# Seven products for the last pair of f blocks in groups 2 and 3, too: S form from the k stage, T forms kept in DRAM

## The chip, the cores and the metric

The kernel runs on one core of a Trainium2 chip. The core has a matrix engine (TensorE, PE in the profile; its weight loads are PEld), VectorE (DVE), ScalarE (ACT), GpSimd (POOL) and SyncE (SP). The last two issue most of the transfers here. Each engine works through its own queue of instructions in order and waits on semaphores for the others. Matmuls write into PSUM, eight banks of 128 x 512 fp32 values; everything else lies in SBUF, or in DRAM.

The metric is the device time of one execution in microseconds. Before the change it is 728.93 us, the median of three runs (728.89 to 728.98).

## The reference

The input x has 2048 tokens of 640 features. The output is a mix, with a gate for each token, of two blocks:

```
g = sigmoid((x * gate_w).sum(-1))
a = linear attention of x (32 heads of 20): phi(q), phi(k), v from x @ wqkv,
    o = (phi(q) @ (phi(k)^T v)) / (phi(q) . sum phi(k)),  a = o @ wo
h = sigmoid(x @ w_gate) * (x @ w_up)        # 640 -> 1536
b = h @ w_down                              # 1536 -> 640
out = g * a + (1 - g) * b
```

All is fp32. The change concerns b in its last step, `h @ w_down`, for half of the tokens.

## The kernel before

**Three matmuls for a product.** The matrix engine takes the type fp32r, which keeps fewer bits of an fp32 value. So each operand is split into a high part (`hi`, a rounded copy that ScalarE makes) and a low part (`lo`, the rest, which VectorE subtracts), and `mm3` issues hi x hi, hi x lo and lo x hi into the same bank. `split` is that pair of instructions.

**Groups and blocks.** The tokens form four groups of 512 (`TG`), which the kernel treats in pairs: the call with `pr = 1` treats groups 2 and 3, that with `pr = 0` groups 0 and 1. The k stage comes first (keys, and the sums that linear attention needs), over chunks of 256 tokens of two groups at once. Then come `q_phase(1)` and `f_phase(1)`, then `q_phase(0)` and `f_phase(0)`, then the attention output. `f_phase` runs over 12 blocks f of 128 hidden features (`FC`). A block has steps 1 to 7, which compute gate and up products for both groups of the pair, and a tail, which forms h = sigmoid(gate) * up.

**Seven products for eight.** Two groups times two weights make a 2 x 2 block product, which is computed with seven products in place of eight from sums of the operands. On the x side these sums are the T forms (`Chunk.sum`, `Chunk.form`: four of them, in SBUF tiles `xt`), on the weight side the S forms. The down products do the same: two f blocks are a pair p, whose h tiles are B11, B12, B21, B22 (first digit: block; second: group), with the sums T1 to T4 of these, and the weights' sums S1 to S4, each for two of the five output blocks at a time (q = 0 and 1); the fifth output block (W and V in the code) takes plain products. `down_pair` is a generator that issues the products of a pair in the order in which the code names them; each `yield` hands back to `f_phase`, which puts a step of the next blocks in between. `new` starts a bank, `go` adds a product to it, `seed` copies a bank to another one on ScalarE, and `out` adds a bank to the sum `tb` on VectorE. For three outputs of the last pair of groups 0 and 1 (`FAR`), `far` copies the bank on ScalarE instead and adds it to `tb` by an accumulating DMA from GpSimd.

**The last pair (blocks 10 and 11).** In groups 0 and 1 it runs behind block 11 with the seven products. In groups 2 and 3, `last_down` runs it with plain products: for ten outputs (five output blocks, two groups) the terms of block 10 and of block 11. The first four outputs start with block 10's terms while block 11's h is being made. `tail_f` makes the h tiles for this. `last_down` also multiplies each output by 1 - g (`scaled`, with `omg` in the tile `ds`) and stores it in `b_dram`.

**Weights.** For groups 2 and 3 the raw w_down block is loaded (`load_d`, tile `dst`), split (`split_d`, tile `wd`) and stored in `wd_dram` for the other groups; for pairs 0 to 4 `queue_ds` and `queue_df` make the S forms (tile `ds`), and store them also. Pair 5's S form is needed for groups 0 and 1 alone; `queue_last_s` makes it in `f_phase(0)`, and `load_last_s` loads it before the last pair.

**x for the next pair.** During the last blocks of `f_phase(1)`, x of groups 0 and 1 is loaded again in two chunks (`other`), and its plain splits (`queue_a`, `queue_b`, `plain_b12`) and T forms (`queue_both`: four sums and four forms for each chunk) are made during the last pair and the first q products. The k stage had made the same T forms for its own use.

**Who sets the order.** All queues are filled in one program order, and `Order` plans it: a model of the time at which TensorE, ScalarE and VectorE come to each instruction. Products are issued in the order of the code. Work on the other two engines is either issued at its place in the code (tails, seeds, outs) or queued by `order.add`; `order.fill` issues queued work where it fits within a slack of TensorE's time, streams with a due time when that comes near, and `order.need(key)` issues all that a product is about to use. The k stage has a list of `kept` items, the pieces of three q weights, that `order.run("qw")` issues one by one at fixed places. `Ring.dma_start` keeps the same kind of account for SP's and GpSimd's transfers.

Of the kernel before, what the change touches and what calls it, by code (L numbers as in the profile page):

```python
# [27 lines left out]
EPS = 1e-6  # L28

# [344 lines left out]
def gated_mix_kernel(ctx: ExitStack, tc: tile.TileContext, xt, xn, wk, wv, wo, wst_q, wst_f, out_t):  # L374
# [160 lines left out]
    class Chunk:  # L535
# [67 lines left out]
        def form(self, t):  # L603
            split(*self.f.t_part(t, self.cs), self.T[t])
# [62 lines left out]
    chunks[0].b12 = (b12h, b12l)  # L667
    wk_st = [op_tile(t, F32) for t in ("xnh", "xnh", "xnl", "pkh", "pkl")]
# [65 lines left out]
    w_dram = {}  # L734
# [311 lines left out]
    for c in range(1, 4):  # L1046
# [496 lines left out]
    wd_dram = {}  # L1543
# [9 lines left out]

    def split_d(n):
# [5 lines left out]
        def rest():  # L1560
            if j == 0:
                wd_dram[p] = dram.tile([P, 2, WF], F32, name=f"wd{p}")
            gp.dma_start(wd_dram[p][:, :, (1 - j) * D:(2 - j) * D], f32(t))
            if p == FC // 2 - 1:
                load_d()
        order.then(rest)
# [45 lines left out]
    WF = 2 * D + 8 * P  # L1612
# [9 lines left out]
    def wf_tile():  # L1622
        return down_pool[1].tile([P, 2, WF], F32R, name="wf", tag="wf")

# [51 lines left out]
    def queue_last_s():  # L1676

        p, w = FC // 2 - 1, 4 * P
        raw = [down_pool[1].tile([P, D], F32, name=n, tag=n)[:, :w] for n in ("mr", "mv")]
        for j in range(2):  # L1680
            sp.dma_start(raw[j], wst_f[2 * p + j, :, 2, :w])
        (a11, a21), (a12, a22) = [r.rearrange("p (q h c) -> h p q c", q=2, h=2) for r in raw]
        at = lambda: max(order.when(r) for r in raw) + 1
        ready = [at]

        def sums(part):
            if part == 0:
                add(a22, a21, a22)
                sub(a21, a11, a21)
            else:  # L1690
                sub(a11, a22, a11)
                sub(a12, a12, a11)

        def form(j):
            t = down_pool[1].tile([P, 2, D], F32R, name="mt", tag="mt")[:, :, :w]
            split(t[:, 0], t[:, 1], raw[j])
            dst = wd_dram[p][:, :, 2 * D + j * w:2 * D + (j + 1) * w]
            ready[0] = lambda: 1e9

            def rest():  # L1700
                gp.dma_start(dst, f32(t))
                ready[0] = lambda: order.when(dst) + 12
            order.then(rest)
        for part in range(2):
            order.add(0, 2 * v_cost(2 * P), lambda part=part: sums(part), "m", at, spare=True)
        for j in range(2):
            order.add(a_cost(w), v_cost(w), lambda j=j: form(j), "m", lambda: ready[0](), spare=True)

    def m_close():
# [13 lines left out]
        other.append(Next(0, 1, xf, CW, c1_x, True))  # L1723

# [50 lines left out]

    def tail_f(f, blk, late=False):
        def t3():
            h_split(f, 0, blk.c11, "v")

        def t4():  # L1780
            act(blk.c12, blk.c12, AF.Sigmoid, "v")
            vec2(blk.c12, blk.c22, blk.c12, OP.mult, "a")

        def t5():
            if late:
                order.add(a_cost(TG), v_cost(TG), lambda: h_split(f, 1, blk.c12, ""), ("hl", f))
            else:
                h_split(f, 1, blk.c12, "v")
        return {3: t3, 4: t4, 5: t5}
# [87 lines left out]
    FAR = [(FC // 2 - 1, 4, 0), (FC // 2 - 1, 0, 0), (FC // 2 - 1, 2, 0)]  # L1877

    def down_pair(pr, p):
# [26 lines left out]
        def far(key, o, g):  # L1906
            if not far_at:
# [7 lines left out]
        def out(key, o, g):  # L1915
            dst = tb[:, o, g]
            if not pr and (p, o, g) in FAR:
# [8 lines left out]

        if p == FC // 2 - 1:
# [18 lines left out]
            go("X0", "S2", "T2")  # L1946
            out("X0", 0, 1)
            go("X1", "S2", "T2", q=1)
            out("X1", 2, 1)
            go("Z0", "S4", "B22")  # L1950
            out("Z0", 0, 1)
            go("Z1", "S4", "B22", q=1)
            out("Z1", 2, 1)
            go("X0", "S3", "T3")
            seed("U0", "rot", "X0")
            out("X0", 1, 1)
            go("X1", "S3", "T3", q=1)
            seed("U1", "rot", "X1")
            out("X1", 3, 1)
            go("W", "w1", "B22")  # L1960
            out("W", 4, 1)
# [5 lines left out]
        if pr:  # L1967
            for j in range(2):
                order.need(("d", ("f", 1, 2 * p + j)))
# [143 lines left out]
    def f_phase(pr, q, hooks={}):  # L2113
# [10 lines left out]
        if pr:  # L2124
            order.plan[pr, FC + 1, "d0"] = at - EARLY
        else:
            for s, n in (("d1", 1), (3, 8), ("d2", 13), ("d3", 15)):
                order.plan[pr, FC + 1, s] = at + mm * n

        def step(f, s):  # L2130
# [24 lines left out]
            if s == 7:  # L2155
                tails[f] = tail_f(f, blk, f == FC - 2) if pr and f >= FC - 2 else tail_s(f, blk) if f < FC - 1 else tail_last(f, blk)
# [28 lines left out]
        for f in range(FC):  # L2185
# [29 lines left out]
            else:  # L2215
                if not pr:
                    queue_t1(f // 2)
# [3 lines left out]
            if f % 2 and f < FC - 1:  # L2221
                queue_t1(f // 2)
                if pr:
                    if f > 1:
                        queue_df(f // 2)
                    queue_d(("f", 1, f + 1))
# [3 lines left out]
            elif not pr:  # L2230
# [10 lines left out]
    def last_down(pr, units):  # L2241
        order.need(("d", ("f", pr, FC - 1)))
        order.need(("hl", FC - 2))
        early = {}
        order.slack_a, order.slack_v = 0.6, 0.8
        if True:
            omg = f32(down_pool[1].tile([P, 2, 8 * P], F32R, name="ds", tag="ds"))[:, :, :TG]
            for g in range(2):
                sp.dma_start(omg[:, g], gate_dram[1, (2 + g) * TG:(3 + g) * TG].partition_broadcast(P))
# [5 lines left out]

        for i in units[:4]:
            g, o = divmod(i, KC)
            early[i] = ps_tile("rot" if (o + g) % 2 else "dd")
            down_term(early[i], pr, FC - 2, o, g, True)
        for i in units:  # L2260
            g, o = divmod(i, KC)
            down_unit(pr, FC - 2, o, g, early.pop(i, None))
            order.add(0, v_cost(TG), lambda i=i: scaled(i), ("tb", i),
                      lambda: order.vec + 0.6, lazy=True)
            order.fill()
        order.slack(False)
# [32 lines left out]
    def load_forms(kind, f, *forms):  # L2299
# [474 lines left out]
```

## Time and profile before

| What | Value |
|---|---|
| median of three runs | 728.93 us |
| the profiled execution | 728.59 us |
| its span | 726.9 us, 10146 instructions |
| granted TensorE clock | 1.000 |
| DMA packets | 74137, 176.95 MB, mean 243 GB/s |

The span is the time between the first and the last instruction of the profiled execution. A row of a timeline has the start and the duration in us, the engine, the line of the code (often that of a helper: 406 to 408 are the three matmuls of `mm3`, 419 is `act`, 423 is `vec2`), the operation, the tile written and those read, the shape, how many instructions the row stands for, and in brackets the idle time before it with what ended it. Durations of instructions that follow each other overlap a little, so the distance between starts tells the pace. The last pair of groups 2 and 3 lies at 392 to 406 us, the last pair of groups 0 and 1 at 645 to 657 us, and the k stage before 135 us.

### The profile page before, as it was taken

The page shows a single profiled execution, that of the slowest core. Times are in us where ns is not written, and L with a number is a line of the kernel's source. Part 1 is how long each engine was busy: PE and PEld are TensorE (multiplying, and loading weights), DVE is VectorE, ACT ScalarE, POOL GpSimd, SP SyncE. Part 2 cuts the span into 40 slices and gives each one's busy share as a digit, 9 for nine tenths or more (in the row PEclk, how much of TensorE's full clock was granted, in tenths as well). Part 3 has the DMA queues.
Part 4 walks back from the last instruction along what each step waited for, and adds up shares of the span by engine and source line. Part 5 has one row for each costly group of instructions (what it writes and reads, how often), then busy time and mean ns, then how long its engine had stood idle before and what let it go on. Part 6 is the DMA issues. An engine that isn't in the chain of part 4 may idle for free.

```text
span 726.9 us, 10146 instructions
## 1 busy us (share of the span) xinstructions
PE 722.2 (99%) x3563; PEld 620.8 (85%) x3563; DVE 573.0 (79%) x1006; ACT 364.0 (50%) x675; POOL 101.2 (14%) x166
## 2 busy tenths in 40 slices
PE   9999999999999999999999999999999999999997
PEld 8999999988888888888888888888888888888886
DVE  6889778987687889898989973447585968698895
ACT  6884649357656653535355363454333232354451
POOL 0211101113212211211210031001000001212000
PEclk9999999999999999999999999999999999999999
DMA  8665658698787866567687289879799695979612
GB/s 258 160 181 111 184 130 252 151 338 295 268 313 259 332 223 232 194 223 253 255 322 273 94 295 331 312 233 311 238 329 358 213 363 169 309 280 291 245 59 102
DMA packets 74137, 176.95 MB, mean 243 GB/s; under 512 B 11834, under 2 KB 35402, under 8 KB 70502
## 3 DMA queue, kind: packets, MB, share of 16 engines
q1 hardware_dynamic: 56102, 111.56, 47.7%
q0 software_dynamic: 17840, 64.57, 25.3%
q8 instruction: 28, 0.46, 0.3%
q14 instruction: 23, 0.19, 0.1%
q10 hardware_dynamic: 144, 0.16, 0.1%
HBM read 105.53 MB, written 64.97 MB: 235 GB/s over the span
## 4 chain that ended last, share of the span: by engine, by line
PE 99%; DVE 0%; issue 0%
PE ch L406 11%; PE ch L407 11%; PE ch L408 11%; PE cc L406 9%; PE cc L407 9%; PE cc L408 9%; PE dd L406 7%; PE dd L408 7%; PE dd L407 7%; PE rot L406 6%; PE rot L407 6%; PE rot L408 6%; PE rot L1505 1%; PE rot L494 0%; PE ch L2576 0%; PE cc L2576 0%
## 5 line engine op out<-in xcount | busy, mean ns | idle before, releaser
L419 ACT ACTIVATE c<-ch 128x512 f32<-128x512 f32 x52 | 31.1, 598 | 90.6 <-PE ch L408 90.5
L423 DVE TENSOR_TENSOR hf<-c,hf 128x512 fp32r<-128x512 f32 x78 | 53.1, 687 | 21.5 <-ACT hf L419 21.2
L419 ACT ACTIVATE hf<-c 128x512 fp32r<-128x512 f32 x78 | 47.7, 625 | 26.0 <-DVE c L423 26.0
L423 DVE TENSOR_TENSOR c<-cc,c 128x512 f32<-128x512 f32 x40 | 27.6, 689 | 34.5 <-PE cc L408 22.3
L406 PE MATMUL ch<-xth,ws 128*128 128x512 f32 x112 | 43.7, 390 | 0.0
L408 PE MATMUL ch<-xth,ws 128*128 128x512 f32 x112 | 43.6, 389 | 0.0
L407 PE MATMUL ch<-xtl,ws 128*128 128x512 f32 x112 | 43.6, 389 | 0.0
L423 DVE TENSOR_TENSOR tb<-rot,tb 128x512 f32<-128x512 f32 (+1 forms) x61 | 39.1, 675 | 3.0 <-PE rot L408 3.0
L423 DVE TENSOR_TENSOR c<-c,c 128x512 f32<-128x512 f32 x50 | 34.4, 688 | 3.3 <-ACT c L419 2.7
L406 PE MATMUL dd<-xrh,wg 128*128 128x512 f32 x90 | 35.2, 391 | 0.0
L408 PE MATMUL dd<-xrh,wg 128*128 128x512 f32 x90 | 35.0, 389 | 0.0
L407 PE MATMUL dd<-xrl,wg 128*128 128x512 f32 x90 | 35.0, 389 | 0.0
L419 ACT ACTIVATE c<-dd 128x512 f32<-128x512 f32 x22 | 13.2, 598 | 41.1 <-PE dd L408 41.1
L423 DVE TENSOR_TENSOR tb<-dd,tb 128x512 f32<-128x512 f32 x40 | 27.4, 686 | 7.7 <-PE dd L408 7.6
L406 PE MATMUL cc<-xbh,ws 128*128 128x512 f32 x84 | 32.7, 389 | 0.0
L408 PE MATMUL cc<-xbh,ws 128*128 128x512 f32 x84 | 32.7, 389 | 0.0
L407 PE MATMUL cc<-xbl,ws 128*128 128x512 f32 x84 | 32.7, 389 | 0.0
L419 ACT ACTIVATE dd<-ch 128x512 f32<-128x512 f32 x22 | 12.8, 582 | 33.6 <-PE ch L408 33.6
L423 DVE TENSOR_TENSOR wst<-wst 128x256 f32<-128x256 f32 (+2 forms) x69 | 27.4, 413 | 1.4
L408 PEld LDWEIGHTS ch<-xth,ws 128*128 128x128 f32 x112 | 21.0, 188 | 4.7
L407 PEld LDWEIGHTS ch<-xtl,ws 128*128 128x128 f32 x112 | 21.0, 188 | 4.2
L406 PEld LDWEIGHTS ch<-xth,ws 128*128 128x128 f32 x112 | 21.0, 188 | 4.1
(663 smaller groups left out, 2362.1 us busy)
## 6 DMA issues: line engine op xcount, KB each, us to landing
wf<-ws POOLq DMA_DIRECT2D x12, 1152.0 KB, 7.6
ws<-wf SPq DMA_DIRECT2D x11, 1152.0 KB, 8.6
wst<-wst_f SPq DMA_DIRECT2D x12, 640.0 KB, 5.1
wf<-wg POOLq DMA_DIRECT2D x12, 640.0 KB, 6.9
wd<-wd POOLq DMA_DIRECT2D x12, 640.0 KB, 8.0
wg<-wf SPq DMA_DIRECT2D x12, 640.0 KB, 5.7
wf<-wd SPq DMA_DIRECT2D x10, 640.0 KB, 9.2
xnst<-xn SPq DMA_DIRECT2D x16, 320.0 KB, 4.2
```

The lines of the kernel that those rows point to most:

```text
L406: nc.tensor.matmul(out, l_hi, r_hi, start=first, stop=False, skip_group_check=True)
L407: nc.tensor.matmul(out, l_hi, r_lo, start=False, stop=False, skip_group_check=True)
L408: nc.tensor.matmul(out, l_lo, r_hi, start=False, stop=last, skip_group_check=True)
L419: nc.scalar.activation(out, src, fn, **kw)
L423: nc.vector.tensor_tensor(out, a, b, op=op)
L1505: nc.tensor.matmul(ps[:w, :w], v[:, m, :w], gt[:, m, c0:c0 + w], start=(m == 0), stop=(m == KC - 1))
```

## The change

- `last_down` and `tail_f` go. Groups 2 and 3 run the last pair through `last_pair` and `down_pair`, as groups 0 and 1 do, in an order of its own: Z0 and Z1 come later, W is finished earlier, R0 and R1 are copies of X0 and X1, so that U0 and U1 start from those, and other banks are used. `FAR` holds for both, with other tiles in groups 2 and 3.
- `queue_ls` makes pair 5's S form in the k stage: two raw loads, four sums in two items, four splits with a store each. They follow the q pieces in the `kept` list, and the places at which the k stage issues these are changed. `queue_last_s` goes. `load_last_s` now runs for both pairs of groups.
- `Chunk.form` stores the T forms of the k stage's second chunk (`chunks[1]`) in `xt_dram`; `load_t` loads them in front of the last pair, and the sums and forms of that chunk are no longer queued.
- The stores of the split weights of blocks 10 and 11 (`last_stores`) and the load of the last raw q block come behind or into the pair; the loads of two q weights come behind the T loads. The scaling by 1 - g (`queue_scaled`) moves into `q_phase(0)`, with its gate rows loaded by GpSimd.

```diff
         def form(self, t):
-            split(*self.f.t_part(t, self.cs), self.T[t])
+            f = self.f.t_part(t, self.cs)
+            split(*f, self.T[t])
+            if self is chunks[1]:
+                order.then(lambda: [gp.dma_start(xt_dram[:, t, i], f32(f[i])) for i in range(2)])
...
+    def queue_ls():
+
+        p, w = FC // 2 - 1, 4 * P
+        wd_dram[p] = dram.tile([P, 2, WF], F32, name=f"wd{p}")
+        raw = qs.tile([P, 2, D], F32, name="qraw", tag="qraw")[:, :, :w]
+        for j in range(2):
+            sp.dma_start(raw[:, j], wst_f[2 * p + j, :, 2, :w])
...
+        def form(j, q):
+            cs = slice(j * w + 2 * q * P, j * w + 2 * (q + 1) * P)
+            t = qs.tile([P, 2, 2 * P], F32R, name="qp", tag="qp", bufs=2)
+            split(t[:, 0], t[:, 1], raw[:, j, 2 * q * P:2 * (q + 1) * P])
+            order.then(lambda: sp.dma_start(wd_dram[p][:, :, 2 * D + cs.start:2 * D + cs.stop], f32(t)))
+        for part in range(2):
+            order.add(0, 2 * v_cost(2 * P), lambda part=part: sums(part), "qw", None, kept=True)
+        for j in range(2):
+            for q in range(2):
+                order.add(a_cost(2 * P), v_cost(2 * P), lambda j=j, q=q: form(j, q), "qw", None, kept=True)
...
-            if c > 1 and n in (2, 5,):
+            for _ in range(({1: 1, 2: 1, 3: 1, 5: 1}, {3: 2, 4: 1, 5: 1})[c - 2].get(n, 0) if c > 1 else 0):
                 order.run("qw")
...
+            if c == 2 and u == 9:
+                queue_ls()
...
+    def load_last_s(pr=1):
+
+        p = FC // 2 - 1
+        if pr:
+            t = down_pool[1].tile([P, 2, 8 * P], F32R, name="ds", tag="ds")
+            DS[p] = [t[:, c] for c in range(2)]
+        else:
+            DS[p] = [x2_tile("ds", F32R).rearrange("p a b -> p (a b)") for _ in range(2)]
+        for c in range(2):
+            sp.dma_start(f32(DS[p][c]), wd_dram[p][:, c, 2 * D:])
...
+    def load_t(t):
+        c = other[1]
+        for i, f in enumerate(c.f.t_part(t, c.cs)):
+            sp.dma_start(f32(f), xt_dram[:, t, i])
...
         if p == FC // 2 - 1:
+            tags = ("cc", "ch") if pr else ("ch", "ch")
             new("W", "dd", "w0", "B11")
-            new("X0", "ch", "A11", "B11")
+            new("X0", tags[0], "A11", "B11")
             seed("V", "dd", "W")
+            yield
             new("X1", "ch", "A11", "B11", 1)
             seed("Y0", "rot", "X0")
             seed("Y1", "rot", "X1")
             yield
-            new("Z0", "cc", "S1", "T1")
-            out("Z0", 1, 1)
-            new("Z1", "cc", "S1", "T1", 1)
-            out("Z1", 3, 1)
+            def zs():
+                new("Z0", "ch" if pr else "cc", "S1", "T1")
+                out("Z0", 1, 1)
+                new("Z1", "cc", "S1", "T1", 1)
+                out("Z1", 3, 1)
+            if not pr:
+                zs()
             go("V", "w1", "B21")
...
             go("W", "w0", "T1")
...
+            if pr:
+                zs()
+                go("W", "w1", "B22")
+                out("W", 4, 1)
+            for q in range(2):
+                go(f"X{q}", "S2", "T2", q=q)
+                if pr:
+                    seed(f"R{q}", "rot", f"X{q}")
+                out(f"X{q}", 2 * q, 1)
+            for q in range(2):
+                go(f"Z{q}", "S4", "B22", q=q)
+                out(f"Z{q}", 2 * q, 1)
+            for q in range(2):
+                x = f"R{q}" if pr else f"X{q}"
+                go(x, "S3", "T3", q=q)
+                seed(f"U{q}", tags[q] if pr else "rot", x)
+                out(x, 2 * q + 1, 1)
+            if pr:
+                order.need((nx[1], 2))
+                order.need(("wg", ("q", 0, 4)))
+            else:
+                go("W", "w1", "B22")
+                out("W", 4, 1)
             go("U0", "A22", "T4")
...
-    def last_down(pr, units):
...
+    def last_pair(pr, tail, between):
+
+        down = down_pair(pr, FC // 2 - 1)
+        order.slack_a = order.slack_v = -9.0
+        if pr:
+            order.need((nx[1], None))
+            next(down)
+        tail[4]()
+        if not pr:
+            next(down)
+        next(down)
+        tail[5]()
+        order.slack_a, order.slack_v = 0.6, 0.8
+        for name in ("T3", "T4"):
+            queue_h(FC // 2 - 1, name)
+        between()
+        for _ in down:
+            pass
+        order.slack(False)
...
-        (FC - 1, 7): [lambda: load_forms("q", 0, 1, 2), queue_b],
+        (FC - 1, 7): [lambda: [load_t(t) for t in (1, 0, 2, 3)], queue_b],
     })
     nx = other
-    for s in (3, 4, 5):
-        tail[s]()
-    for c in other:
-        order.add(a_cost(2 * CW), v_cost(2 * CW), c.plain_b12, (nx[1], "plain"))
-    queue_both(nx)
-    queue_q(4)
-    last_down(1, range(2 * KC))
...
+    def next_x():
+        load_d()
+        load_forms("q", 0, 1, 2)
+        for c in other:
+            order.add(a_cost(2 * CW), v_cost(2 * CW), c.plain_b12, (nx[1], "plain"))
+        w = 2 * CW
+        c = other[0]
+        for ns, t, k in (((0, 1, 2), 1, 3), ((), 0, 4), ((), 2, 5), ((3,), 3, 6)):
+            for m in ns:
+                order.add(0, v_cost(w), lambda m=m: c.sum(m), None, lambda: c.at)
+            order.add(a_cost(w), v_cost(w), lambda t=t: c.form(t), (nx[1], k))
+        queue_q(4)
+    last_pair(1, tail, next_x)
+    for fn in last_stores:
+        fn()
```

More of the change, by code (lines that the diff above doesn't have):

```diff
@@ L1674, in queue_m @@
         order.add(a_cost(D), v_cost(D), fn, "m", lambda: order.when(raw) + 2, spare=True)
[L1676 to L1707, printed above, removed]
     def m_close():
@@ L1906, in far @@
         def far(key, o, g):
-            if not far_at:
+            if not far_at and order_pr[0]:
+                t = f32(wd_tile())
+                far_at.extend((t[:, 0], t[:, 1], down_pool[1].tile([P, D], F32, name="far", tag="dst", bufs=2)))
+            elif not far_at:
                 far_at.extend(down_pool[1].tile([P, D], F32, name="far", tag=n) for n in ("mr", "mv"))
@@ L1945, in down_pair @@
             go("W", "w0", "T1")
[L1946 to L1961, printed above, removed]
+            if pr:
[18 more added lines that the diff above has]
+                order.need(("wg", ("q", 0, 4)))
+            else:
+                go("W", "w1", "B22")
+                out("W", 4, 1)
             go("U0", "A22", "T4")
@@ L2229, in f_phase @@
                 step(f + 1, 2)
-            elif not pr:
+            else:
                 tail_last(f, blocks[f])[3]()
@@ L2254, in scaled @@
             gp.dma_start(b_dram[:, o, g], tb[:, o, g])
[L2256 to L2262, printed above, removed]
+        for i in range(2 * KC):
             order.add(0, v_cost(TG), lambda i=i: scaled(i), ("tb", i),
-                      lambda: order.vec + 0.6, lazy=True)
-            order.fill()
-        order.slack(False)
+                      lambda: max(order.vec + 0.6, order.when(omg)), lazy=True)
     order.need((nx[1], 2))
@@ L2526, in gated_mix_kernel, with next_p @@
     })
-    down = down_pair(0, FC // 2 - 1)
-    order.slack_a = order.slack_v = -9.0
-    tail[4]()
-    next(down)
-    tail[5]()
-    order.slack_a, order.slack_v = 0.6, 0.8
-    for name in ("T3", "T4"):
-        queue_h(FC // 2 - 1, name)
-    load_p(groups[1])
-    for g in groups[:2]:
-        load_b(g)
-    for _ in down:
-        pass
-    order.slack(False)
+    def next_p():
+        load_p(groups[1])
+        for g in groups[:2]:
+            load_b(g)
+    last_pair(0, tail, next_p)
     for u in range(KC):
```

90 lines of the change are left out of this document (40 added, 50 removed).

## The prediction

> **What bounds the kernel now.** I read the page's busy times first, then the waits of TensorE, then the windows and timelines around the last pair of groups 2 and 3, because the page alone does not say how full the other engines are there.
>
> ```profile
> PE 722.2 (99%) x3563; PEld 620.8 (85%) x3563; DVE 573.0 (79%) x1006; ACT 364.0 (50%) x675; POOL 101.2 (14%) x166
> ...
> PE rot L494 <- PEq L2765: 0.8, 1, 0.8
> ...
> 380.00:400.00 20.00, 20.00 (x90) 16.56 (x89) 18.96 (x32) 9.68 (x18) 1.42 (x3) 1.00 0.77 286
> 400.00:420.00 20.00, 20.00 (x95) 16.80 (x94) 18.28 (x30) 8.40 (x15) 0.56 (x1) 1.00 0.32 114
> 420.00:440.00 20.00, 20.00 (x90) 16.56 (x89) 14.20 (x23) 11.45 (x21) 9.35 (x18) 1.00 0.89 302
> ```
>
> Busy times and waits say the same: TensorE is the bound from end to end, and its one wait (0.8 us) is the first instruction. The windows (columns PE, PEld, DVE, ACT, POOL, clock, DMA share, GB/s) say what is second: around the change VectorE works 18.96 and 18.28 of 20 us. So a matmul taken out is time gained, and whatever makes VectorE or a load late there gives it back.
>
> The stretch that is replaced, in TensorE's timeline:
>
> ```profile
> 389.76 0.39 PE L408 MATMUL cc<-hf,ds 128*128 128x512 f32 x1
> ...
> 391.80 0.39 PE L408 MATMUL cc<-xbh,ws 128*128 128x512 f32 x1
> 392.03 0.39 PE L406 MATMUL dd<-hf,wd 128*128 128x512 f32 x1
> ...
> 405.63 0.39 PE L406 MATMUL ch<-xah,wg 128*128 128x512 f32 x1
> ```
>
> last_down runs from 392.03 to 405.63: 20 products of three matmuls, so 60 in 13.60 us, 0.2267 us each, without a gap.
>
> **The matmuls.** down_pair issues 18 products for the last pair (W three times, V, Y0, Y1, R0, R1, U0, U1 once, X0, X1, Z0, Z1 twice), so 54 matmuls in place of 60: 6 x 0.2267 = 1.36 us less, 0.187%. Nothing else on TensorE changes, in the k stage or in groups 0 and 1 (the same 18 products in the same order). Since TensorE has no gap to close, 1.36 us is all that can be gained, and the rest of the sum is what is given back. The Trainium skill ("TensorE: Matmul & The Clock Gate", section "Part 1: The HAM clock gate") gives N/2.4 GHz + 2.5 ns between starts, 215.7 ns for 512 columns; by that the six are worth an estimated 1.29 us and the sum would be 0.07 us longer. The trace differs, with 226.7 ns, and decides.
>
> **A model for the stretch.** The same seven products already run at the end of groups 0 and 1, so their hand-overs have rows (TensorE, ScalarE, VectorE):
>
> ```profile
> 654.50 0.39 PE L408 MATMUL ch<-hf,ds 128*128 128x512 f32 x1
> ...
> 646.13 0.63 ACT L419 ACTIVATE c<-c 128x512 f32<-128x512 f32 x1 [2.30 <-DVE c L423]
> 646.67 0.58 ACT L419 ACTIVATE dd<-dd 128x512 f32<-128x512 f32 x1
> 647.18 1.03 ACT L419 ACTIVATE rot<-ch 128x512 f32<-128x512 f32 x2
> ...
> 654.99 1.26 ACT L419 ACTIVATE rot<-ch 128x512 f32<-128x512 f32 x2 [2.50 <-PE ch L408]
> ...
> 645.41 0.69 DVE L423 TENSOR_TENSOR c<-cc,c 128x512 f32<-128x512 f32 x1 [0.48 <-PE cc L408]
> ```
>
> The sigmoid of c12 starts 0.72 us after the c12 sum (645.41 to 646.13); the copies that seed a bank follow it 0.54 us later and each other at 0.51, and take 0.58; a seed starts 0.49 us after its source's last matmul (654.50 to 654.99). One product takes 0.68 us. So in the new order, with t = 0 at 392.03, the products are due at: W 0, X0 0.68, X1 1.36, V 2.04, Y0 2.72, Y1 3.40, W with T1 4.08, Z0 (S1) 4.76, Z1 5.44, W with B22 6.12, X0 and X1 (S2) 6.80 and 7.48, Z0 and Z1 (S4) 8.16 and 8.84, R0 9.52, R1 10.20, U0 10.88, U1 11.56, end 12.24.
>
> **U0 behind R0.** U0 is a copy of R0, and only R1 stands between them; in groups 0 and 1 W with B22 stands there too. R0's last matmul starts at 9.97, the copy at 10.46, and it ends at 11.04, where U0 is due at 10.88: 0.16 and the signal. Bounds 0 (R1 late for another reason) and 0.3; I take 0.2. U1 then comes in step.
>
> **Y0 and Y1 behind the sigmoid.** In groups 2 and 3 ScalarE's queue holds V's seed, the sigmoid, then the seeds of Y0 and Y1, so a late sigmoid holds Y0. It waits for VectorE's c12 sum:
>
> ```profile
> 391.83 0.69 DVE L423 TENSOR_TENSOR tb<-cc,tb 128x512 f32<-128x512 f32 x1
> 392.43 0.69 DVE L423 TENSOR_TENSOR hf<-c,hf 128x512 fp32r<-128x512 f32 x1
> 393.03 0.69 DVE L423 TENSOR_TENSOR cx<-cc,cx 128x512 f32<-128x512 f32 x1
> ```
>
> VectorE, at 0.60 us for an operation in a row, is already late: the sum could start at 392.19 (391.80 + 0.39) and starts at 393.03. Ahead of it come T1's difference and low part (1.20) and no longer block 10's second low part (0.60): 393.63. Then the sigmoid at 394.35 and Y0's seed from 394.89 to 395.47, where Y0 is due at 394.75: 0.72 us. With the sum at 393.03 it is 0.12; with the sum at once, 0; with T1's two steps added and nothing dropped, 1.3. The planner puts off optional splits when VectorE is late, so I take 0.4, between 0.12 and 0.72. X0 now takes the cc bank of pair 4's Z1, whose sum into tb ends at 392.52, X0 being due at 392.71; the same lateness meets both, and I count it once.
>
> **B22, T2, T3, T4.** With the c12 sum at 393.3, t = 1.3: sigmoid 2.0, product 2.7, T2 and T4 to 4.5, low parts of B22 and T2 at 5.1 and 5.7, due at 6.12 and 6.80. So 0, bounded by 0.6 where the sum is at its latest.
>
> **The S form's load.** It takes the ds tile, so it waits for 389.76 + 0.39 = 390.15, and Z0 wants it at 396.79. It is two transfers of 512 KB. The nearest rows of the DMA view (KB each, median us to landing), then the windows:
>
> ```profile
> xst<-xt SPq DMA_DIRECT2D x2, 640.0 KB, 4.1
> ...
> ds<-wd SPq DMA_DIRECT2D x2, 512.0 KB, 7.6
> ...
> ds<-gate_dram SPq DMA_DIRECT2D x2, 256.0 KB, 9.7
> ...
> 386.00:390.00 4.00, 4.00 (x20) 3.30 (x19) 4.00 (x8) 2.16 (x4) 0.00 (x0) 1.00 0.24 94
> 394.00:398.00 4.00, 4.00 (x20) 3.30 (x19) 3.14 (x6) 3.18 (x7) 0.00 (x0) 1.00 1.03 414
> ```
>
> The first is a load of the k stage, the second this very form in groups 0 and 1 under load, the third one behind other transfers. The DMA engines move 414 GB/s when full, so 384 KB over the first row's 640 are 0.95 us more: 5.05 us, landed at 395.2, 1.6 us early. The ends are 394.25 (4.1 us) and 399.85 (9.7 us, 3.06 late). I take 0, nearest the first row: at 386 to 390 the DMA engines are nearly idle (share 0.24), the stores of the last two weights are put behind the pair, and the T loads stand behind this load on SP's queue. With 7.6 us it lands at 397.75, 0.96 late, which would make 729.1 of the sum below. The Trainium skill ("DMA: Bandwidth & Descriptors", section "Anatomy of one DMA — SWDGE (gpsimd) path") has 2.0 us + bytes at 436 GB/s, an estimated 4.4 us for this load: no stall, the sum as below, against 729.1 by the row of 7.6. For the 640 KB row the rule gives 3.5 and the trace shows 4.1, so it is a little short.
>
> **What leaves, and what is queued elsewhere.** The T forms of the second chunk (four sums, four high and four low parts) leave the time after the pair:
>
> ```profile
> 409.19 2.14 DVE L423 TENSOR_TENSOR wst<-wst 128x512 f32<-128x512 f32 x3
> ```
>
> With the fourth sum and four low parts at 0.60 that is 5.1 us of VectorE. TensorE covered it: 0 by itself. Against it VectorE gets, earlier, inside the pair, four differences, three more low parts and one more sum into tb: 8 x 0.60 = 4.8 us. The ten scalings of tb move into the q products and behind them; 420 to 440 has 5.8 us free. SP's queue gets the S and T loads (10 transfers, 3.1 MB) ahead of the last raw q block (0.3 MB): at 414 GB/s these are 8.3 us, landed by about 400.5 with 2 us of start, and its split is due at its own product, t = 12.24 + 5 x 0.68 = 15.6, so at 407.7: 0, bounded by 1. POOL gets two weight stores, three sums into tb by DMA and the gate rows, and is busy 0.56 of 20 us there; nothing of TensorE waits for these.
>
> In the k stage four sums and four forms are added, and two pieces of q come earlier:
>
> ```profile
> L423 DVE TENSOR_TENSOR qp<-qraw,qp x10: 280/418/422, 56.7 to 110.3; 128x256 fp32r<-128x256 f32 x7, 128x128 fp32r<-128x128 f32 x3
> ...
> 108.98 0.49 DVE L423 TENSOR_TENSOR kb<-cc,kb 128x322 f32<-128x322 f32 x1 [3.88 <-ACT kb L419]
> ...
> 136.31 0.63 ACT L419 ACTIVATE xth<-xst 128x512 fp32r<-128x512 f32 x1 [7.80 <-DVE xst L423]
> ```
>
> 8 x 0.42 = 3.3 us of VectorE, against 3.88 idle just there. The last two forms stand behind block 7, and SP's loads of the next x wait for their stores to let the pool go, by some 4 us; ScalarE's 7.80 us of idle time behind those splits cover it, and if that cover were gone it is 1 us. POOL's eight T stores meet a queue that is busy 14% of the time. So 0, bounded by 1.0. Groups 0 and 1 lose the form that they made, which lay under matmuls: 0.
>
> **The sum.** -1.36 + 0.2 + 0.4 = -0.76 us. The profiled execution took 728.59 (span 726.9) and would take 727.83. The median of the runs, 728.93, stands 0.34 above it and gives 728.17, so 728.2.
>
> **The rivals.** *VectorE sets the pace of the pair.* Could no sum lag, its 4.8 us more, less the idle time of the two windows (1.04 and 0.8 of the 1.72), would stretch the pair by 3.0: -1.36 + 3.0 = +1.6, so 730.5, slower. For it: 18.96 of 20. Against: the last six sums into tb free banks that TensorE wants only 2 us or more later, and 5.1 us leave just behind. It decides from 2.82 us of stalls. *The S load lands late:* at 9.7 us it is -1.36 + 3.06 + 0.2, so 730.8, and it decides from a landing at 399.4. Against: the idle DMA engines. *No stall at all:* 727.57, still within 0.2%. *Both hand-overs at their dear ends with some lateness of the load:* 1.45 to 2.8 us of stalls, 729.0 to 730.4. *Faster by over 0.2%* would need 0.1 us more than the six matmuls, and no row has it.
>
> **How the numbers follow.** 0.2% (1.46 us) is about what a measurement of this kernel can tell from no change. Forecast, stalls of 0 to 1.45 us (727.5 to 729.0): 0.65. Dear hand-overs: 0.14. VectorE's pace 0.09, the late load 0.05, the k stage 0.02, together slower: 0.16. Faster: 0.05. Same is 0.65 + 0.14 = 0.79. The range goes from 727.5 (no stall) to 730.6 (VectorE's pace).
>
> **What would show it.** Right: 54 matmuls between block 11 and the q products, gaps of 0.1 to 0.8 us ahead of Y0 and U0 that ScalarE releases, none ahead of Z0, none in the k stage. Wrong: a gap ahead of Z0 that a DMA releases, gaps ahead of Z0's and Z1's second products or of B22 and T2 that VectorE releases, or a gap in the k stage.

## The result, and the profile after

The changed kernel takes 735.31 us (median of 12 runs, 730.86 to 737.82) against 728.93 us for the kernel before, run beside it (12 runs). The ratio is 1.0072, with a 95% interval of 1.0051 to 1.0093: slower, where no change was forecast, and 4.7 us above the range. Its runs lie 7 us apart, most of those of the kernel before within 0.5 us. The profiled execution took 736.47 us, 1.2 above the median, with a span of 734.8 us against 726.9. Two executions among those of the experiments, of 2586 and 1878 us, are slow ones and stay out of the ratios and medians below.

The first line of the page:

```profile
PE 725.5 (99%) x3557; PEld 620.8 (84%) x3557; DVE 573.7 (78%) x1008; ACT 369.1 (50%) x686; POOL 107.9 (15%) x177
```

Six matmuls fewer, and yet TensorE is busy for longer: a share of busy time doesn't tell a matmul at full clock from one at half, and since a row of 0.39 us is shown where matmuls start 0.23 us apart, it hides short waits as well. So the two timelines of TensorE were laid beside each other, matmul by matmul. The changed kernel falls behind by 4.1 us between 53 and 59 us, by another 2.1 between 179 and 193, wins 0.3 in the pair itself, loses 0.35 at the products behind it and 1.7 between 626 and 645. That is, within 0.1 us, the 7.9 us of the two spans.

**The k stage (+4.1).** Of the changed kernel, TensorE's timeline, ScalarE's, and SP's (start, duration, what ended the idle time before); below them the windows, with the granted clock, the DMA share and GB/s as the last three columns:

```profile
52.80 0.31 PE L409 MATMUL rot<-pkh,xnl 128*128 128x320 f32 x1
54.92 0.41 PE L407 MATMUL rot<-pkh,xnh 128*128 128x320 f32 x1 [1.80 <-ACT xnh L420]
...
56.45 0.47 PE L408 MATMUL dd<-pkl,xnh 128*128 128x320 f32 x1
56.72 0.47 PE L409 MATMUL dd<-pkh,xnl 128*128 128x320 f32 x1
```

```profile
54.13 0.74 ACT L420 ACTIVATE xnh<-xnst 128x640 fp32r<-128x640 f32 x1 [5.04 <-DMA xnst<-xn]
```

```profile
44.05 12.02 SPq L364 DMA_DIRECT2D xnst<-xn  x4
```

```profile
48.00:52.00 4.00, 4.00 (x29) 4.00 (x29) 2.18 (x4) 0.82 (x2) 0.22 (x1) 1.00 1.04 351
52.00:55.00 3.00, 1.20 (x9) 0.93 (x7) 0.10 (x1) 0.87 (x2) 0.00 (x0) 1.00 1.10 320
55.00:56.00 1.00, 0.70 (x3) 0.44 (x4) 0.79 (x2) 1.00 (x4) 0.00 (x0) 0.92 1.10 271
56.00:57.00 1.00, 1.00 (x5) 1.00 (x6) 0.73 (x1) 0.97 (x3) 0.00 (x0) 0.50 0.72 159
...
59.00:60.00 1.00, 1.00 (x8) 1.00 (x7) 1.00 (x3) 1.00 (x3) 0.23 (x1) 0.87 0.22 36
```

Read it backwards. TensorE waits for ScalarE's split of xnst, and ScalarE for one of the three loads of xn that SP issued between 44.05 and 47.15 us. (The row of SP holds four loads, 12.02 us from first to last, 7.22 before. The fourth goes out at 55.75, when the split has freed its tile: it follows from the stall and is no cause of it.) Then the clock falls: it is granted at 0.92 in the slice that starts at 55 us, at 0.50 in the three from 56 to 59 and at 0.87 in the next, which makes 3.4 us at half clock. The matmuls, 0.15 us apart until then, come 0.27 apart. The wait costs 2.0 us, a shorter one for VectorE behind it 0.5, and the half clock some 1.6.

What the loads met stands in GpSimd's timeline and in the DMA view from 36 to 60 us (KB each, median us from issue to landing):

```profile
37.88 1.20 POOL L364 DMA_DIRECT2D zacc<-kb  x1 [4.78 <-DVE ksl L424]
38.61 1.09 POOL L364 DMA_DIRECT2D xt_dram<-xth  x1
...
42.63 0.80 POOL L364 DMA_DIRECT2D xt_dram<-xtl  x1
```

```profile
xst<-xt SPq DMA_DIRECT2D x2, 640.0 KB, 7.3
xnst<-xn SPq DMA_DIRECT2D x4, 320.0 KB, 10.6
xt_dram<-xth POOLq DMA_DIRECT2D x4, 256.0 KB, 7.2
```

GpSimd stood 4.78 us before its zacc transfer, for VectorE. Behind it the stores of the first two T forms collected, whose low parts VectorE had finished at 32.5 and 34.9 us. When it came free, these and the other two forms' stores, eight with 2 MB, went out between 38.6 and 43.4 us, beside the loads of x and just ahead of those of xn: 7.3 and 10.6 us to landing, before 4.1 and 5.2.

**179 to 193 us (+2.1).** TensorE, then ScalarE, in the changed kernel:

```profile
184.11 0.50 PE L407 MATMUL ch<-xth,wu 128*128 128x512 f32 x1 [0.39 <-ACT c L420]
193.05 0.50 PE L407 MATMUL ch<-xth,ws 128*128 128x512 f32 x1 [1.16 <-ACT c L420]
```

```profile
191.22 0.63 ACT L420 ACTIVATE qe<-c 128x512 f32<-128x512 f32 x1 [2.89 <-DMA p_dram<-qe]
```

ScalarE wants a qe tile that the store of p_dram has not yet released. Why it has not is read below, from the S form alone.

**The pair of groups 2 and 3 (-0.3).** The stretch from the first matmul of the pair to the first of the q products, as one window, then TensorE and ScalarE at its two hand-overs:

```profile
398.27:411.55 13.28, 12.94 (x56) 9.90 (x54) 13.21 (x22) 9.14 (x18) 4.11 (x5) 1.00 1.04 342
```

```profile
400.87 0.39 PE L409 MATMUL dd<-hf,wd 128*128 128x512 f32 x1
401.27 0.50 PE L407 MATMUL rot<-hf,wd 128*128 128x512 f32 x1
...
409.34 0.39 PE L409 MATMUL rot<-hf,ds 128*128 128x512 f32 x1
410.05 0.50 PE L407 MATMUL cc<-hf,wd 128*128 128x512 f32 x1 [0.33 <-ACT cc L420]
```

```profile
400.10 0.64 ACT L420 ACTIVATE cx<-cx 128x512 f32<-128x512 f32 x1 [0.37 <-DVE cx L424]
...
409.42 0.58 ACT L420 ACTIVATE cc<-rot 128x512 f32<-128x512 f32 x1 [1.05 <-DVE tb L424]
```

It takes 13.28 us in place of 13.60 (13.26 to 13.30 in every kernel below that has the pair so), where 54 matmuls without a gap take 12.24. The first matmul of Y0 comes 0.17 us late and the next 0.10; U0's 0.48 and 0.11; nothing is late at Z0, so the S form's load was in time. VectorE is busy for 13.21 of the 13.28 us.

**626 to 645 us (+1.7).** VectorE, TensorE and SP in the changed kernel:

```profile
637.72 0.69 DVE L428 SCALAR_TENSOR_TENSOR pl<-pl,fac 128x512 f32<-128x512 f32 x1 [3.93 <-DMA pl<-p_dram]
```

```profile
643.71 0.50 PE L407 MATMUL cc<-hf,wf 128*128 128x512 f32 x1 [0.23 <-DVE tb L424]
```

```profile
618.67 2.16 SPq L364 DMA_DIRECT2D wf<-wd  x3
620.93 2.20 SPq L364 DMA_DIRECT2D pl<-p_dram  x2
623.22 15.77 SPq L364 DMA_DIRECT2D fac<-fac_dram  x8
```

The same rows of SP in the kernel before:

```profile
610.65 2.49 SPq L363 DMA_DIRECT2D fac<-fac_dram  x4
613.24 1.00 SPq L363 DMA_DIRECT2D ws<-wf  x1
614.29 1.88 SPq L363 DMA_DIRECT2D wf<-wd  x3
616.21 1.32 SPq L363 DMA_DIRECT2D pl<-p_dram  x2
```

Nothing that the change adds is here, but the order is another. On SP the first four loads of fac stood ahead of ws, now eight stand in a row behind pl. On VectorE the scaling of pl stood behind two sums into tb (at 628.40 and 631.81 us), now it stands ahead of them. And pl comes no earlier for it: issued at 620.93 in place of 616.21, it lands after 16.8 us in place of 15.4, so 6.1 us later, as late as the whole program by then. VectorE stands 3.93 us for it, the sums wait behind, and TensorE's banks come free late.

### The profile page after: what moved, and what is told of

Same layout as the page of the kernel before. It is cut to its first block, busy times and chain, and to the rows that moved or that the text cites. A ratio compares the mean times of both kernels' runs of the same rounds, so it can differ in the third digit from the quotient of the medians.

```text
span 734.8 us, 10212 instructions
## 1 busy us (share of the span) xinstructions
PE 725.5 (99%) x3557; PEld 620.8 (84%) x3557; DVE 573.7 (78%) x1008; ACT 369.1 (50%) x686; POOL 107.9 (15%) x177
## 4 chain that ended last, share of the span: by engine, by line
PE 83%; DVE 6%; DMA 5%; issue 2%; ACT 1%; POOL 1%; POOLq 0%; DVEq 0%; ACTq 0%
PE ch L407 9%; PE ch L408 9%; PE ch L409 9%; PE cc L407 7%; PE cc L409 7%; PE cc L408 7%; PE dd L408 6%; PE dd L407 6%; PE dd L409 6%; PE rot L409 5%; PE rot L407 5%; PE rot L408 4%; DMA pl<-p_dram 2%; DMA xnst<-xn 1%; DVE tb L424 1%
## 5 line engine op out<-in xcount | busy, mean ns | idle before, releaser
L424 DVE TENSOR_TENSOR tb<-rot,tb 128x512 f32<-128x512 f32 (+1 forms) x58 | 37.1, 673 | 3.0 <-PE rot L409 3.0
L424 DVE TENSOR_TENSOR tb<-dd,tb 128x512 f32<-128x512 f32 x36 | 24.7, 685 | 6.5 <-PE dd L409 6.5
L424 DVE TENSOR_TENSOR wst<-wst 128x256 f32<-128x256 f32 (+1 forms) x65 | 24.6, 395 | 1.4
L424 DVE TENSOR_TENSOR tb<-cc,tb 128x512 f32<-128x512 f32 x36 | 24.4, 683 | 1.0 <-PE cc L409 1.0
```

Of the source, the lines that this page charges most:

```text
L424: nc.vector.tensor_tensor(out, a, b, op=op)
```

## The experiments

Two theories at first. **A:** the burst of T stores in the k stage is the loss. **B:** the pair in seven products, with VectorE so full, is the loss. The late rows gave a third, **C:** the S form's move re-orders work elsewhere.

### The changed kernel again

No edit.

> The changed kernel once more, unchanged, so that its profile can be laid beside the first one. Theory A (the eight stores of 256 KB of the T forms, issued by GpSimd within 5 us in the k stage, hold up the loads of x's next chunk): the 2 us gap of TensorE at 54.9 us and the granted clock of 0.50 at 56 to 59 us are there again, the median is 735 (733 to 738). Theory B (the seven-product pair and its S form cost the time, the k-stage gap was an accident of the one profiled execution): the gap at 54.9 is gone in this profile though the time is again 735.

735.03 us (732.50 to 737.97), ratio 1.0082 (1.0052 to 1.0113). The gap is there again, 2.88 us from one matmul's start to the next, and so is the clock of 0.50. The stall of 1.3 us at 193 is not: that one comes in some executions only.

### The T stores issued by SP

```diff
-                order.then(lambda: [gp.dma_start(xt_dram[:, t, i], f32(f[i])) for i in range(2)])
+                order.then(lambda: [sp.dma_start(xt_dram[:, t, i], f32(f[i])) for i in range(2)])
```

> The changed kernel with one word changed: the eight stores of the T forms are issued by SP at the point where each form is made, not by GpSimd behind its zacc transfer. The order of every other instruction on all engines is the same. Theory A: the stores go out one by one from 32 us on, where the DMA engines were nearly idle, the loads of x and xn then land in 4 to 5 us, the gap at 54.9 and the half clock go, and the end comes about 4 us earlier than in the changed kernel: 731 (730 to 732.5). Theory B: nothing of the 6.4 us is from these stores: 735.

732.64 us, ratio 1.0050 (1.0034 to 1.0067). SP and ScalarE of this kernel:

```profile
32.23 0.33 SPq L364 DMA_DIRECT2D xt_dram<-xth  x1
...
41.47 0.32 SPq L364 DMA_DIRECT2D xt_dram<-xtl  x1
41.84 1.27 SPq L364 DMA_DIRECT2D xst<-xt  x2
```

```profile
50.01 0.74 ACT L420 ACTIVATE xnh<-xnst 128x640 fp32r<-128x640 f32 x1 [0.46 <-DMA xnst<-xn]
```

The same 2 MB, spread from 32 to 41.5 us, and the stall of the k stage is gone, the half clock with it. A holds there. But the end came only 2.4 us earlier than beside it in the kernel above, and just outside what A expected: the late stall has grown to some 2.5 us, so a part was given back 580 us later. The edit changes two things at once, the moment of the stores and the queue that issues them, and no run separates the two.

### The T part undone, and the T part alone

The first takes xt_dram, its stores and its loads out of the changed kernel, the second puts them into the kernel before:

```diff
-            if self is chunks[1]:
-                order.then(lambda: [gp.dma_start(xt_dram[:, t, i], f32(f[i])) for i in range(2)])
...
-        (FC - 1, 7): [lambda: [load_t(t) for t in (1, 0, 2, 3)], queue_b],
+        (FC - 1, 7): [queue_b],
```

> The changed kernel with the T part alone undone: no T form is stored or loaded, and the four T forms of x's second chunk are formed anew beside the pair of groups 2 and 3, as in the kernel before. Theory A: no gap at 54.9, no half clock, and the late stall at 633 to 645 goes too if it came with the re-planned loads; but the pair now carries four more sums and four more forms (about 4.8 us of VectorE), which may stall TensorE there: 729 to 731.5. Theory B: the loss stays, 735 or more.

> The kernel before with the T part alone done: the eight stores in the k stage, the eight loads ahead of the last pair, no T form of the second chunk formed anew; the pair of groups 2 and 3 stays in eight products and no S form is made in the k stage. Theory A: the gap at 54.9 and the half clock appear here: 732 to 734, slower than before by 3 to 5 us. Theory B: 728 to 729, as before or a little faster.

Undone: 732.34 us, ratio 1.0044 (1.0030 to 1.0059). Alone: 733.64 us, ratio 1.0060 (1.0036 to 1.0084), with 3.53 us from start to start at the gap, the half clock, and no other new stall. So the T part as written costs the kernel before 5 us, all of it in the k stage. But without it the changed kernel is still 3.7 us slower than the kernel before, which A had not expected. This needs a second cause, and B and C both offer one.

### The S form alone, and the pair alone

The S form alone is the kernel before with queue_ls in the k stage and queue_last_s taken out of groups 0 and 1. The pair alone is the kernel without T part with the reverse edit:

```diff
-            if c == 2 and u == 9:
-                queue_ls()
...
+        (7, 4): [queue_last_s],
```

> The kernel before with the S form part alone done: the S form of the last pair is made in the k stage and kept in DRAM, the S form's making late in groups 0 and 1 is gone; the pair of groups 2 and 3 stays in eight products and all T forms are formed anew. Theory C (taking that making out of groups 0 and 1 lets the program's own planner put the first four loads of fac behind the loads of pl, eight in a row, so that VectorE stands behind a late pl and TensorE behind VectorE's sums): gaps of 1 to 2.5 us between 620 and 640 and ACT's wait on wo_sb near 175: 730 to 732. Rival, that the late stall comes from the pair or the T forms: no gap after 600, 728.3 to 729.2.

> The kernel before with the pair of groups 2 and 3 in seven products alone: no T form is kept, no S form is made in the k stage (its making in groups 0 and 1 is back), and the pair reads as a stand-in the S form of the pair of f blocks before it, so the output is not the reference's. Theory A with C: six matmuls fewer (-1.36 us) against hand-overs of 0.9 to 1.1 us at Y0 and U0 and up to 1.6 us at the first products of the next stage, where VectorE still forms T: 728 to 730, no gap at 54.9, none after 600. Theory B (the pair itself costs the time): 732 or more.

S form alone: 732.35 us, ratio 1.0042 (1.0027 to 1.0057). Pair alone: 730.07 us, ratio 1.0015 (1.0005 to 1.0024), and its ten runs lie within 0.8 us. The first is 0.35 us above what C expected, the second 0.07 above what A and C did. B falls as the main loss: the pair costs 1 us, and not through its own stretch, which takes 13.28 us here too, but behind it. TensorE in the kernel with the pair alone:

```profile
420.47 0.40 PE L407 MATMUL cc<-xth,ws 128*128 128x512 f32 x1
422.32 0.50 PE L408 MATMUL cc<-xtl,ws 128*128 128x512 f32 x1 [1.45 <-DVE xtl L424]
```

VectorE, full through the pair, is late with the T forms by 1.6 us; keeping them in DRAM does help there. C is what costs. With the S form alone, ScalarE, then SP and TensorE late in groups 0 and 1:

```profile
187.18 0.63 ACT L420 ACTIVATE qe<-c 128x512 f32<-128x512 f32 x1 [3.31 <-DMA p_dram<-qe]
```

```profile
616.93 1.49 SPq L364 DMA_DIRECT2D pl<-p_dram  x2
618.52 15.87 SPq L364 DMA_DIRECT2D fac<-fac_dram  x8
```

```profile
639.02 0.50 PE L407 MATMUL cc<-hf,wf 128*128 128x512 f32 x1 [0.23 <-DVE tb L424]
```

Why the q products suffer begins at the end of the k stage. SP in the kernel before, then with the S form alone; below them two windows of the kernel before and the same two with the S form alone:

```profile
114.04 2.11 SPq L363 DMA_DIRECT2D xz<-xt  x2
```

```profile
117.28 1.34 SPq L364 DMA_DIRECT2D wd<-qp  x2
...
124.27 1.03 SPq L364 DMA_DIRECT2D xz<-xt  x2
```

```profile
120.00:140.00 20.00, 20.00 (x138) 20.00 (x137) 19.91 (x35) 9.20 (x16) 3.57 (x3) 1.00 0.82 209
140.00:180.00 40.00, 40.00 (x227) 34.74 (x226) 33.76 (x71) 26.62 (x51) 9.36 (x17) 1.00 0.92 302
```

```profile
120.00:140.00 20.00, 20.00 (x138) 20.00 (x137) 18.29 (x32) 8.82 (x14) 3.47 (x3) 1.00 0.79 231
140.00:180.00 40.00, 39.86 (x225) 34.44 (x224) 35.46 (x74) 27.40 (x52) 9.06 (x18) 1.00 0.92 302
```

The S form's own steps on VectorE are done by 117.6 us. But the pool that holds its pieces closes before xz, a part of x for the q products, is loaded. So SP waits for the last stores of the S form to land, up to 4.2 us at a time, and the load starts 10.2 us later. ScalarE comes to the first two splits of xz 2.8 and 5.6 us later, each behind that load. VectorE, which had hardly an idle moment from 120 to 140 us, is busy for 1.6 us less there: the order has changed, and it stands 1.23 us for TensorE at 126.9 with the splits of x behind that. These 1.6 us come back as 1.7 us more work in the q products. The stores of qe, 256 KB each, take 7.0 us to landing at the median (165 to 192 us), before 5.3.

The same holds in all eight profiles with the S form in the k stage: the load of xz starts at 123.07 us or later and the stores of qe take 6.1 to 7.5 us. The six others load xz at 114 to 115 us (one, 6 us late by then, at 120) and have 3.9 to 5.3. This chain is read from the traces. No run moves that load alone, so its share and that of the changed order are not told apart.

All eight profiles of kernels with the S form in the k stage have a gap of 0.2 to 0.7 us near 180 to 184, and three of them one of 1.3 to 1.8 us at 187 to 193 as well. None of the six without it has either.

### The late order put back

In the kernel with T stores on SP, and then in the one with the S form alone, the planner's number for a scaling of pl:

```diff
-            order.add(0, v_cost(TG), lambda u=u: pq_scale(g, u), ("sc", g), lambda u=u: order.when(t[u]) + 1, lazy=True)
+            order.add(0, v_cost(TG), lambda u=u: pq_scale(g, u), ("sc", g), lambda u=u: order.when(t[u]) + 4, lazy=True)
```

> The changed kernel with the T stores issued by SP, and one number of the planner changed: a scaling of pl may be put 4 us after its modelled landing, no more 1 us. SP's order late in groups 0 and 1 is then that of the kernel before (four loads of fac ahead of ws, four behind pl). Theory C: the gaps of 2.5 us at 624 to 641 of the run with T stores on SP alone go, 730 (729.3 to 731). Rival, that the stall is from late data whatever the order: 732.6 again.

> The kernel before with the S form part alone, and the planner's number for pl set to 4 us, so that the loads of fac stand late in groups 0 and 1 as in the kernel before. What is left of the S form part is the VectorE and ScalarE work in the k stage, that is, the stall between 179 and 190: 0.2 us where ScalarE finds its qe tile free, 2 us where the store of p_dram lands late: 729.3 to 731.3, no gap after 600. Rival, that the S form part costs only through the late loads: 728.7 to 729.1.

SP's order is then again four loads of fac, ws, wf, pl, four of fac. With the T stores on SP: 730.18 us, ratio 1.0017 (1.0007 to 1.0027), and of the gaps between 620 and 645 one of 0.45 us is left, behind a late wf. So the order made the late stall, 2 of 2.5 us. (The number moves the scaling on VectorE and the loads of fac together; that the scaling counts is read from VectorE's wait for pl.) With the S form alone: 731.57 us, ratio 1.0027 (1.0011 to 1.0044), a little above what was expected; its ten runs lie between 729.71 and 733.85. The profiled one is a short one, 729.87, and has 0.73 us at 180, 0.23 at 626 and no stall at 187. That the longer ones have the stall at 187 to 193 fits, but no profile of one was taken.

### The change without its S form

The pair alone plus the T part, its stores on SP.

> The pair of groups 2 and 3 in seven products and the T forms kept in DRAM with their stores issued by SP; no S form in the k stage (its making in groups 0 and 1 is back), and the pair reads as a stand-in the S form of the pair of f blocks before it, so the output is not the reference's. This is the change without its S form part and without GpSimd's stores. If the losses add up as the gaps say: -1.36 us of matmuls, 0.27 at Y0, 0.59 at U0, 0.1 to 0.4 at the next stage instead of the 1.6 of the run with the pair alone: 728.4 to 729.2, no gap at 54.9, 179 to 193 or after 600. Rival, that the T stores cost time wherever they are issued: 730.5 or more.

728.87 us, ratio 0.9992 (0.9982 to 1.0002). No gap at 54.9, between 179 and 193, or after 600; what is left is 0.28 at Y0, 0.58 at U0 and 0.45 at the q products. The parts add up: -1.36 + 1.3 of hand-overs, and the execution starts its first products 0.7 us late.

### U0 in another bank

In the kernel with T stores on SP and the order put back:

```diff
-                seed(f"U{q}", tags[q] if pr else "rot", x)
+                seed(f"U{q}", ("dd", "ch")[q] if pr else "rot", x)
```

> The kernel of the run before this one, with the seed of U0 put into a bank of dd, which the W product's sum frees 0.6 us earlier than X0's sum frees its bank of cc. If the hand-over at U0 costs what its gap shows (0.59 us), the end comes 0.4 to 0.6 us earlier than without: 729.5. If VectorE sets the pace of the pair, the gap only moves to U1 or to the next stage and the time stays within 0.15 us.

TensorE of this kernel:

```profile
405.85 0.39 PE L409 MATMUL rot<-hf,ds 128*128 128x512 f32 x1
406.23 0.50 PE L407 MATMUL dd<-hf,wd 128*128 128x512 f32 x1
...
406.79 0.40 PE L409 MATMUL dd<-hf,wd 128*128 128x512 f32 x1
407.15 0.50 PE L407 MATMUL ch<-hf,wd 128*128 128x512 f32 x1
```

The gap at U0 fell from 0.60 to 0.25 us and U1 got one of 0.24: most of it moved, as a hand-over does when VectorE behind it is full. The stretch takes 13.19 us, 0.1 less. The time, 731.58 us, is above the 729.5 that a gain would have given and above the kernel without the edit, but says nothing on the bank, since its profile has the stall at 189 (1.46 us).

### The S form at the start of groups 2 and 3

If the k stage is the wrong place, another may do: two loads ahead of the other down weights, sums and forms in the first block, where no pair is down yet. T stores and order as above; then the same with U0's other bank.

```diff
+    d_loads = [("s", 1, FC - 2), ("s", 1, FC - 1)] + entries[1:] + [("q", 0, 4)]
...
+        (0, 3): [queue_first_s],
```

> The changed kernel with three parts moved: the T stores are issued by SP; the S form of the last pair is made at the start of the products of groups 2 and 3, where no pair is down yet, from two loads ahead of the other down weights, and not in the k stage; the planner's number for pl is 4 us. Theory: VectorE and ScalarE have room there, so nothing is lost at 54.9, at 179 to 193 or after 600, and what is left is the pair with its hand-overs: 728.5 to 729.2, as in the run with a stand-in S form, or up to 0.15% faster than the kernel before. Rival: the new place has no room either, or the later loads of the down weights are late: 730 or more with a new gap between 195 and 250.

> The kernel of the run before this one with the seed of U0 in a bank of dd. The earlier run of this edit showed the gap at U0 go from 0.60 to 0.25 us and a new one of 0.24 us at U1, so VectorE's last sums of the pair set the pace: 0.1 us faster, not to be told apart from none. Rival: the edit is worth 0.5 us and the earlier run lost it elsewhere.

730.50 us, ratio 1.0022 (1.0013 to 1.0031), and 730.67 us, ratio 1.0026 (1.0017 to 1.0035). The rival was right: TensorE loses 1.5 us between 211 and 227, the last 0.7 of it for a weight that VectorE splits later than before (one row of the first):

```profile
227.02 0.50 PE L409 MATMUL dd<-hf,wd 128*128 128x512 f32 x1 [0.43 <-DVE wd L424]
```

Another 1 us goes at 627 to a late wf. U0's bank is again worth 0.1 us in the stretch (13.18 against 13.30) and nothing that can be told in the time. No version that makes the S form itself beat the kernel before; the one that comes level reads a stand-in.

## Why the prediction was wrong, point by point

- **The matmuls, -1.36:** right. 54 matmuls, and no other product changed.
- **Y0, 0.4 (0.12 to 0.72):** right in mechanism, 0.27 measured: the sigmoid waits for VectorE, and Y0's seed behind it.
- **U0, 0.2 (0 to 0.3):** too small, 0.59. The step took R0's end as what the seed waits for. ScalarE waited 1.05 us for VectorE instead: X0's last sum still held the bank of cc. A seed waits for its source and for its bank, and only one was counted.
- **B22, T2, the S form's load, 0:** right. The load landed 4.8 us after its issue, where 5.05 were taken. (The estimate of 4.4 beside it goes by a rule for the "SWDGE (gpsimd) path", and this load is SP's.)
- **SP's queue, 0, bounded by 1:** 0.35 in the profiled execution, within the bound, but at another load than the one that was priced: wg, issued at 415.15 us, lands after 6.9 us (before 4.4), since the DMA engines, at a share of 0 to 0.49 there before, are at 1.05.
- **The k stage, "So 0, bounded by 1.0":** here the prediction failed, twice. "POOL's eight T stores meet a queue that is busy 14% of the time" took a share over the whole span for a place in time. What counts is when the eight come out, which GpSimd's own wait for VectorE decided, and what SP loads then. It cost 4.1 us with the half clock (5 us alone). And of the S form the step priced the wrong cost. Its 3.3 us on VectorE, "against 3.88 idle", did run by 117.6 us, if not in that one idle row, which lies before a single sum. What failed is the cover for "SP's loads of the next x": the step let ScalarE's 7.80 us of idle time cover a delay of "some 4 us". In the kernel with the S form alone the load of xz started 10.2 us later, ScalarE's splits of it came up to 5.6 us later, and VectorE, busy for 19.91 of 20 us there before, did 1.6 us less from 120 to 140 us and had them to do in the q products, where 0.2 to 2.1 us were lost.
- **Groups 0 and 1, "which lay under matmuls: 0":** wrong, 1.0 to 2.5 us. The removed form had cost nothing, but this program's order is planned, and taking work out moved two VectorE steps, the scalings of pl, ahead of pl's landing and of the sums that free TensorE's banks.
- **The rivals:** the k stage had a chance of 0.02 and was the case. That VectorE sets the pace is half true: it was busy for 13.21 of 13.28 us, but this cost 0.9 us, not 3.0, until the T forms are added to it (1.6 more). The upper end of the range, 730.6, is 0.1 above what VectorE's pace gave and 0.2 below the rival of the late load.

The sum as it should have stood for the profiled execution, from its rows: -1.36 + 1.04 in the pair, +4.1, +2.1, +0.35 and +1.7, so +7.9 (7.87 measured).

## What to carry to other kernels

Price a moved transfer by the moment of its departure, not by the share of its queue: look for what the issuing engine waits on ahead of it, since transfers that collect behind a wait leave as a burst, and for the loads that others have due just then. Ask also what a tile or pool that closes later holds up, and follow that through every engine behind it, not only the one with idle time. Work that is taken out of a planned order needs the same look as work that is put in, at each queue's order and not at its sums alone. Where an engine is already busy nearly all the time, an algorithm that saves matmuls by more of its sums has to show a place with room for each of them; here 1.36 us of matmuls could not pay for one small form made elsewhere.

## What was not expected of the hardware

A pause of TensorE can cost twice. After 2.12, 2.88 and 3.53 us from one matmul's start to the next the granted clock fell to 0.50 for 3.4 us, and the matmuls came 0.27 us apart, not 0.15; after 1.99 us (the S form alone) and 1.85 us (the pair alone) it stayed at 1.00. Whether the length of the pause decides or its place in time, these five do not show. The window behind the pause of the S form alone:

```profile
189.00:190.00 1.00, 0.99 (x4) 0.86 (x5) 0.79 (x2) 1.00 (x1) 0.51 (x1) 1.00 0.77 313
```

The Trainium skill ("TensorE: Matmul & The Clock Gate", section "Part 1: The HAM clock gate") has the half rate after an idle window of about 3.4 us, and the full rate again after as much sustained work. The length of the half clock agrees with that; its start does not, since here pauses of little over 2 us were enough.

The half clock does not come in every execution: the mean granted clock is 0.996 to 0.998 in five of the changed kernel's twelve runs (735.95 to 737.82 us) and 1.000 in the other seven (730.86 to 735.90). The 4.1 us of the k stage are those of a profiled execution that had it; how long the pause was in the seven is not shown.

Also, nearly every first matmul after a pause is followed by the next some 0.34 us later, not 0.23: a wait of 0.48 us costs 0.59.
